# A gated unit whose output sums run over two chunks in PSUM, with moved small steps around it

## The chip, the cores and the metric

The kernel runs on one core of one Trainium2 chip. The metric is the device time of the whole program in microseconds; the median of three runs is 434.72 us (434.70 to 435.04). The core has five engines with their own instruction streams: TensorE (PE, matmuls), VectorE (DVE), ScalarE (ACT), GpSimd (POOL) and SyncE (SP, which here only issues DMAs). Engines wait for one another through semaphores; each takes its own instructions in order.

## The reference

Three stages follow one another, all in float32 at their borders. The gated unit, which the change is mostly about, is the last.

```
# 1 linear attention with a decaying state, per head (2 x 8 heads, 768 steps, 48 wide)
cur = (u * k_t) outer v_t
y_t = r_t @ (state + cur);  state = w * state + k_t outer v_t
# 2 top-1 mixture of experts on 1536 tokens of 384: 8 experts, 1024 wide, a capacity per expert
h = relu(x_e @ w1[e]);  out = gate * (h @ w2[e])
# 3 gated unit, d_ff = 1536
g = x @ w_gate;  val = x @ w_val
out = (g * sigmoid(g) * val) @ w_out
```

The unit's weights arrive as float64.

## The kernel before

**Attention.** The 1536 tokens are 12 tiles of 128. For tile i, SP loads r and k twice: transposed (`load_T`, three buffers) and by token (`load_rk`, three buffers). DVE multiplies the transposed pair by powers of the decay (`decay`, line 258, one multiplication of 128x1024 whose inputs are both in SBUF; for tile 0 in two halves). POOL does two multiplications of 128x384 per tile, again with both inputs in SBUF: `diag_pool` (r times k, line 263) and `keys_pool` (the keys for the state, line 267). `products(i)` issues both and then the load of the tile three ahead into the buffer that they read; `decayed(i)` issues the decay and the transposed load. DVE finishes the diagonal (`diag_u`, line 270, and `diag_sum`, line 275), ACT spreads it on the diagonals of a tile (`diag_act`, line 288), PE computes scores (line 299, into PSUM buffers of which there are three, two per tile), and DVE copies the scores under a mask into the same tile (`masked`, line 307). A short prologue, written out by hand, does tiles 0 to 2 in part; then a loop follows. In the loop some POOL products are told to wait for a decay (`behind`, an explicit dependency, with the reason that both read two operands in SBUF).

**Experts.** Loads of w1 and w2 are split into a high and a low part (fp32r) by ACT and DVE; PE multiplies.

**Gated unit.** `gated` runs over six chunks c of 256 hidden columns, over two pairs p of token groups (a group is 384 tokens), and over two halves f of a chunk: 24 blocks, which the text calls (c,p,f). A block computes gate and value for both groups of its pair from sums of inputs and sums of weights: eleven products of three fp32r matmuls (high by high, high by low, low by high), collected in four PSUM banks named pa, pb, pc, pd. In order they are: the first gate product (into pb, copied to pa by ACT, line 1263), S1 (into pd, copied to m5 by ACT, line 1271), S2 (onto pb; then DVE adds pb and m5 into pc, line 1276), two products onto pa (then SiLU on ACT), S3 (onto pb; then DVE adds pb and m5 into pd, line 1285), two onto pc (then SiLU, line 1291), one onto pd (then DVE multiplies by the gate, line 1297), two onto pb (then DVE multiplies, line 1303). Each result is split by `halves`: ACT casts the high part (line 1231), POOL subtracts to get the low part (line 1232; in the last block DVE does that). The second result of a block is split at the start of the next block.

The output sums of a chunk, three tiles of 128 tokens per group, are handed out as fill: `sum_tile` issues six matmuls (lines 1204 to 1206) for a tile, at up to three places of a block, before S1, before S3 and before the product onto pd; there is none at the first place until block (0,1,1). `added` (lines 1208 to 1219) then evicts the bank: ACT copies it for the first chunk, DVE adds it to a tile in SBUF for the others (line 1213), and after the last chunk POOL sends the rows out by an indirect DMA (line 1215). Only one set of tiles, group 2 of the second pair, is summed over the last two chunks in PSUM, with twelve matmuls each.

Beside this, the float64 weights of the coming chunk are converted in steps that `background` hands out (lines 828 to 921): DVE shifts and merges bits (lines 837, 843, 849), ACT casts the high part, POOL subtracts the low part (line 876). `STEPS` says how many of these steps, and how many of the second pair's input steps (`x_pair`, lines 1137 to 1176), a block takes at its three places. A step in the list takes its place in every engine's stream that it uses. After the last block `at_end` loads a flag (whether a rare case needs the general path) on every engine; the flag is made from PE's count in an output bank and one DVE operation (lines 1322 to 1330).

Of the kernel before, what the change touches and what calls it, by code (L numbers as in the profile page):

```python
# [74 lines left out]

class Kernel:
# [14 lines left out]
    def run(self):  # L91
        tc, nc = self.tc, self.nc
        with ExitStack() as top, tc.manual_schedule():
# [7 lines left out]
            with ExitStack() as ex:  # L101
# [10 lines left out]
                self.wff = [self.weights_ff(mp, 0)]  # L112
# [16 lines left out]
    def attention(self, st):  # L129
# [281 lines left out]
        def products(i):  # L411
            diag_pool(i)
            keys_pool(i)
            load_rk(i + NB)
# [9 lines left out]
        products(1)  # L424
        warm(WARMS[0])
        scores(0)
        decayed(1)
        load_v(3, 1)
# [7 lines left out]
        products(2)  # L436
# [5 lines left out]
        decayed(2)  # L442
        state_pe(1)
# [370 lines left out]
    def weights_ff(self, pool, i):  # L814

        shapes = {"in": [P, NW, 256], "out": [P, 2, DM]}
        return {m: [pool.tile(shape, F32R, name=f"w{m}_{q}{i}") for q in ("hi", "lo")] for m, shape in shapes.items()}
# [7 lines left out]
    def convert(self, m, c):  # L825
# [5 lines left out]
        wide = lambda: self.wff[c % 2]["in" if m != "w_out" else "out"]  # L831
# [305 lines left out]
    def x_pair(self, p):  # L1137
# [9 lines left out]
        def low(at, src, n):  # L1147
            nc.vector.tensor_sub(xl[:, at:at + n], src, xh[:, at:at + n].bitcast(F32))
# [28 lines left out]
    def gated(self, st, at_end=lambda: None):  # L1177
# [6 lines left out]
        self.wff.append(self.weights_ff(wk, 1))  # L1184
        self.xb.append(self.x_rooms(wk, 1))
# [4 lines left out]
        sums, todo = [], []  # L1190
# [3 lines left out]
            (0, 1, 0): ((0, 2), (0, 1), (0, 2)),  # L1194
        }

        def tile_of(c, n, parts):

            po = ps_o.tile([P, DM], F32, name="po", tag="po")
            ts_ = slice(n % NTT * P, (n % NTT + 1) * P)  # L1200
            for i, (at, f, halves_, j) in enumerate(parts):
                ah, al = halves_[j]
                wh, wl = (w[:, f] for w in self.wff[at % 2]["out"])
                nc.tensor.matmul(po, lhsT=ah[:, ts_], rhs=wh, start=(i == 0), stop=False)  # L1204
                nc.tensor.matmul(po, lhsT=ah[:, ts_], rhs=wl, start=False, stop=False)  # L1205
                nc.tensor.matmul(po, lhsT=al[:, ts_], rhs=wh, start=False, stop=(i == len(parts) - 1))  # L1206
            return lambda: added(c, n, po)

        def added(c, n, po):
            if c == 0:  # L1210
# [3 lines left out]
            if c == NC - 1:  # L1214
# [13 lines left out]
        def halves(sg, eng=nc.gpsimd):  # L1228
            h_ = wk.tile([P, TG], F32R, name="ah", tag="ah", bufs=12)
            l_ = wk.tile([P, TG], F32R, name="al", tag="al", bufs=12)  # L1230
            nc.scalar.copy(h_, sg)  # L1231
            eng.tensor_sub(l_, sg, h_.bitcast(F32))  # L1232
            return h_, l_

        def block(c, p, f, steps, tiles):
# [4 lines left out]
            room = lambda name: wk.tile([P, TG], F32, name=name, tag=name, bufs=2)  # L1240
# [6 lines left out]
            def product(ps, wi, xi, first=False):  # L1247
                wh, wl = (w[:, wi, fs] for w in self.wff[c % 2]["in"])
# [4 lines left out]
            def opened(ps):  # L1253

                if c == p == f == 0:
                    nc.tensor.matmul(
                        ps, lhsT=self.wff[0]["in"][0][:, GATE, fs], rhs=self.xb[0][0][:, X11], start=True, stop=True
                    )
# [41 lines left out]
            parts = [None, halves(gate1, low_eng)]  # L1300
# [4 lines left out]
            def rest():  # L1305
                parts[0] = halves(gate0, low_eng)
# [3 lines left out]

        prep, before = self.x_pair(1), []
        for c in range(NC):
            for p in range(2):
                blocks = [block(c, p, f, STEPS.get((c, p, f), ((0, 1), (0, 1), (0, 2))), c > 0 or p > 0 and f > 0) for f in range(2)]
# [7 lines left out]
                if c == NC - 1 and p == 1 and not self.guarded:  # L1322
                    how_many = ps_o.tile([P, DM], F32, name="po", tag="po")
                    nc.tensor.matmul(
                        how_many[:, 0:1], lhsT=self.ones_bf, rhs=low_any, start=True, stop=True
                    )
                    nc.vector.scalar_tensor_tensor(
                        out=self.rare_i, in0=how_many[0:1, 0:1], scalar=0.0, in1=self.rare_f,
                        op0=ALU.is_gt, op1=ALU.add,
                    )  # L1330
                for j in (1, 0):
                    parts = [(c, f, blocks[f], j) for f in range(2)]

                    if (p, j) == (1, 0) and c == NC - 2:
                        held = parts
                        continue
                    if (p, j) == (1, 0) and c == NC - 1:
                        parts = held + parts
                    sums += [(c, (2 * p + j) * NTT + tt, parts) for tt in range(NTT)]
        before.pop()()  # L1340
        while sums:
            if len(sums) == 1:
                at_end()
# [4 lines left out]
    def general(self):  # L1348
# [86 lines left out]
        self.wff, self.xb = self.wff[0:1], self.xb[0:1]  # L1435
# [58 lines left out]
```

## Time and profile before

| | us |
|---|---|
| median of 3 runs | 434.72 |
| profiled execution, its own time | 434.78 |
| its span, first to last instruction | 433.0 |
| PE busy in the span | 417.6 |
| DVE busy | 330.9 |
| ACT busy | 256.8 |
| POOL busy | 158.9 |

The profile is of one execution. Its time stands 0.06 us over the median of the runs; 1.8 us of it lie outside the span. PE's matmuls overlap in the records, so the distance from one start to the next says more than a duration. A hole in PE's work is a distance that is larger than that of its neighbours.

### The profile page before, as it was taken

The page shows a single profiled execution, that of the slowest core. Times are in us where ns is not written, and L with a number is a line of the kernel's source. Part 1 is how long each engine was busy: PE and PEld are TensorE (multiplying, and loading weights), DVE is VectorE, ACT ScalarE, POOL GpSimd, SP SyncE. Part 2 cuts the span into 40 slices and gives each one's busy share as a digit, 9 for nine tenths or more (in the row PEclk, how much of TensorE's full clock was granted, in tenths as well). Part 3 has the DMA queues.
Part 4 walks back from the last instruction along what each step waited for, and adds up shares of the span by engine and source line. Part 5 has one row for each costly group of instructions (what it writes and reads, how often), then busy time and mean ns, then how long its engine had stood idle before and what let it go on. Part 6 is the DMA issues. An engine that isn't in the chain of part 4 may idle for free. (4 is left out here: it accounts for less than half of the span.)

```text
span 433.0 us, 8410 instructions
## 1 busy us (share of the span) xinstructions
PE 417.6 (96%) x3105; PEld 401.1 (93%) x3105; DVE 330.9 (76%) x648; ACT 256.8 (59%) x557; POOL 158.9 (37%) x149
## 2 busy tenths in 40 slices
PE   8999999999999999999999999999999999999991
PEld 7888889999999999999899999999999999999981
DVE  6999996878788988888887578888779778543440
ACT  2688875565876777766766765466546555433300
POOL 5846643111021110000148544445436535323541
PEclk9999999999999999999999999999999999999996
DMA  7999933899999999503012121212221220000221
GB/s 262 350 339 341 408 123 107 246 308 335 326 294 271 260 286 252 193 1 75 0 62 73 52 79 37 88 52 78 75 78 62 75 73 2 0 2 0 74 108 47
DMA packets 23938, 63.78 MB, mean 147 GB/s; under 512 B 4816, under 2 KB 8272, under 8 KB 23888
## 3 DMA queue, kind: packets, MB, share of 16 engines
q1 hardware_dynamic: 21248, 57.43, 41.2%
q0 software_dynamic: 1920, 4.73, 3.0%
q10 hardware_dynamic: 720, 1.00, 1.0%
q8 instruction: 26, 0.43, 0.4%
q14 instruction: 24, 0.20, 0.1%
HBM read 55.67 MB, written 7.48 MB: 146 GB/s over the span
## 5 line engine op out<-in xcount | busy, mean ns | idle before, releaser
L1232 POOL TENSOR_TENSOR al<-gate,ah 128x384 fp32r<-128x384 f32 x46 | 49.8, 1086 | 141.4 <-ACT ah L1231 141.3
L753 DVE TENSOR_TENSOR wlo<-raw,whi 128x768 fp32r<-128x768 f32 x60 | 56.9, 957 | 10.8 <-ACT whi L752 9.4
L942 PE MATMUL py<-hc,whi 128*128 128x448 f32 x192 | 62.3, 379 | 0.0
L953 PE MATMUL A<-xc,whi 128*128 128x224 f32 x336 | 57.2, 276 | 0.3 <-DVE xc L769 0.3
L953 PEld LDWEIGHTS A<-xc,whi 128*128 128x128 f32 x336 | 51.0, 192 | 0.9 <-DVE xc L769 0.5
L943 PE MATMUL py<-hc,wlo 128*128 128x224 f32 x192 | 51.0, 266 | 0.0
L752 ACT CAST whi<-raw 128x768 fp32r<-128x768 f32 x60 | 49.7, 839 | 1.7 <-PE py L942 1.7
L1204 PE MATMUL po<-wout_hi,ah 128*128 128x384 f32 x144 | 48.7, 338 | 0.3 <-DVE x L1213 0.2
L1206 PE MATMUL po<-wout_hi,al 128*128 128x384 f32 x144 | 48.9, 340 | 0.0
L1205 PE MATMUL po<-wout_lo,ah 128*128 128x384 f32 x144 | 48.5, 337 | 0.0
L953 PE MATMUL A<-xc,wlo 128*128 128x224 f32 x168 | 45.9, 273 | 0.0
L1231 ACT CAST ah<-gate 128x384 fp32r<-128x384 f32 x48 | 24.7, 515 | 34.2 <-DVE gate L1297 33.1
L1251 PE MATMUL A<-xbh,win_hi 128*128 128x384 f32 x120 | 40.8, 340 | 1.1 <-DVE gc L1276 0.9
L1251 PE MATMUL A<-xbh,win_lo 128*128 128x384 f32 x120 | 40.3, 336 | 0.0
L1251 PE MATMUL A<-xbl,win_hi 128*128 128x384 f32 x120 | 40.3, 336 | 0.0
L1020 POOL DMA_INDIRECT ids<-tok,by_expert x12 | 13.9, 1156 | 69.8 <-DMA ids<-tok,by_expert 63.5
L942 PEld LDWEIGHTS py<-hc,whi 128*128 128x128 f32 x192 | 36.1, 188 | 3.0
L943 PEld LDWEIGHTS py<-hc,wlo 128*128 128x128 f32 x192 | 36.7, 191 | 0.0
L1213 DVE TENSOR_TENSOR x<-x,po 128x384 f32<-128x384 f32 x57 | 30.9, 544 | 6.7 <-PE po L1206 6.7
L972 ACT ACTIVATE hc<-A 128x224 fp32r<-128x224 f32 x64 | 23.2, 362 | 21.2 <-PE A L953 17.3
L288 ACT ACTIVATE AT<-ident,c 128x128 f32<-128x128 f32 x96 | 30.2, 393 | 4.6 <-DVE c L275 4.5
L953 PEld LDWEIGHTS A<-xc,wlo 128*128 128x128 f32 x168 | 32.3, 192 | 0.0
(208 smaller groups left out, 1070.9 us busy)
## 6 DMA issues: line engine op xcount, KB each, us to landing
raw<-in_w SPq DMA_DIRECT2D x62, 384.0 KB, 8.3
rkT<-in_rkT SPq DMA_DIRECT2D x12, 512.0 KB, 5.9
rk<-in_rk SPq DMA_DIRECT2D x12, 384.0 KB, 5.3
raw<-in_w_gate SPq DMA_DIRECT2D x6, 768.0 KB, 4.9
raw<-in_w_val SPq DMA_DIRECT2D x6, 768.0 KB, 4.3
raw<-in_w_out SPq DMA_DIRECT2D x6, 768.0 KB, 4.9
x_disp<-zero SPq DMA_DIRECT2D x8, 336.0 KB, 6.5
xr<-x_disp SPq DMA_DIRECT2D x8, 336.0 KB, 6.9
```

The costliest lines, as they stand in the source:

```text
L288: nc.scalar.activation(AT[i][:, j, hp], ident, AF.Copy, scale=cc[i][:, j, hp:hp + 1])
L752: nc.scalar.copy(h_, raw)
L753: nc.vector.tensor_sub(l_, raw, h_.bitcast(F32))
L942: nc.tensor.matmul(ps[:, 0:2 * BLK], lhsT=wh, rhs=xc, start=first, stop=False, skip_group_check=True)
L943: nc.tensor.matmul(ps[:, HI], lhsT=wl, rhs=xc[:, HI], start=False, stop=last, skip_group_check=True)
L953: self.nc.tensor.matmul(ph[:, HI], lhsT=w[:, k, fs], rhs=x[1][:, k, half], start=(k == 0 and i == 0), stop=(k == KD - 1 and i == 2),)
L1204: nc.tensor.matmul(po, lhsT=ah[:, ts_], rhs=wh, start=(i == 0), stop=False)
L1205: nc.tensor.matmul(po, lhsT=ah[:, ts_], rhs=wl, start=False, stop=False)
L1206: nc.tensor.matmul(po, lhsT=al[:, ts_], rhs=wh, start=False, stop=(i == len(parts) - 1))
L1213: nc.vector.tensor_add(acc[:, n], acc[:, n], po)
L1232: eng.tensor_sub(l_, sg, h_.bitcast(F32))
L1251: nc.tensor.matmul(ps, lhsT=w, rhs=x, start=first and i == 0, stop=False, skip_group_check=True)
```

## The change

Output sums: instead of one eviction per chunk, each group's tile stays open in PSUM over two chunks. `held(c, j)` says which group of a pair waits for the next chunk: the first of the pair after even chunks, the second after odd ones, none after the last. `sum_tile` now issues one piece, six matmuls of one chunk, and evicts after the last piece of a tile. The high and low parts of held groups get their own seven buffers each, the others four each in place of twelve; the output weights get three buffers instead of two, and m5 one instead of two.

Smaller parts: the low parts of the first block are kept back until the inputs of the second pair are split, with an explicit dependency on that split. In block (0,1,0) one conversion step moves from the second place to the third. The flag is made ahead of the last block, in one of the pa-tile banks. In the attention, `products(1)` and `products(2)` stand behind the decays of tiles 1 and 2, and their first product waits for them.

```diff
-        def products(i):
-            diag_pool(i)
+        def products(i, after=None):
+            op = diag_pool(i)
+            if after:
+                behind(op, after)
             keys_pool(i)
             load_rk(i + NB)
...
-        products(1)
         warm(WARMS[0])
         scores(0)
         decayed(1)
+        products(1, decays[1])
...
-        products(2)
         scores(1)
         outputs(0)
...
         decayed(2)
+        products(2, decays[2])
         state_pe(1)
         products(3)
...
-            (0, 1, 0): ((0, 2), (0, 1), (0, 2)),
+            (0, 1, 0): ((0, 1), (0, 2), (0, 2)),
...
+        def held(c, j):
+            return c % 2 == j and c < NC - 1
...
         def sum_tile():
-            if sums:
-                todo.append(tile_of(*sums.pop(0)))
+            if not sums:
+                return
+            c, n, pieces, i, end = sums.pop(0)
+            if i == 0:
+                opened_sum.append(ps_o.tile([P, DM], F32, name="po", tag="po"))
+            po = opened_sum[-1]
+            ts_ = slice(n % NTT * P, (n % NTT + 1) * P)
+            for f, (h_, l_) in enumerate(pieces[i][1]):
+                at = pieces[i][0]
+                wh, wl = (w[:, f] for w in self.wout[at % 3])
+                nc.tensor.matmul(po, lhsT=h_[:, ts_], rhs=wh, start=(i == 0 and f == 0), stop=False)
+                nc.tensor.matmul(po, lhsT=h_[:, ts_], rhs=wl, start=False, stop=False)
+                nc.tensor.matmul(po, lhsT=l_[:, ts_], rhs=wh, start=False, stop=(end and f == 1))
+            if end:
+                first, last = pieces[0][0] == 0, c == NC - 1
+                todo.append(lambda: added(n, po, first, last))
...
+        def halves(sg, eng, hold, long):
+            tags, bufs = (("kh", "kl"), 7) if long else (("ah", "al"), 4)
+            h_, l_ = (wk.tile([P, TG], F32R, name=t, tag=t, bufs=bufs) for t in tags)
             nc.scalar.copy(h_, sg)
-            eng.tensor_sub(l_, sg, h_.bitcast(F32))
+            low = lambda: eng.tensor_sub(l_, sg, h_.bitcast(F32))
+            held_lows.append(low) if hold else low()
...
+            hold = c == p == f == 0
+            if held_lows and not prep:
+                for low in held_lows:
+                    self.tc.add_manual_dep(
+                        low().ins, self.token_low.ins.name, AFTER, reason="both read two operands in SBUF"
+                    )
+                held_lows.clear()
+            long = [held(c, j) or (c, j) == (NC - 1, 0) for j in range(2)]
...
+        def flagged():
+            how_many = self.pa_tile()
+            nc.tensor.matmul(how_many[:, 0:1], lhsT=self.ones_bf, rhs=low_any, start=True, stop=True)
+            nc.vector.scalar_tensor_tensor(
+                out=self.rare_i, in0=how_many[0:1, 0:1], scalar=0.0, in1=self.rare_f, op0=ALU.is_gt, op1=ALU.add,
+            )
...
                 for j in (1, 0):
-                    parts = [(c, f, blocks[f], j) for f in range(2)]
...
+                    pieces = kept.pop((p, j), []) + [(c, Parts(blocks, j))]
+                    if held(c, j):
+                        kept[p, j] = pieces
                         continue
...
+                    for tt in range(NTT):
+                        sums += [(c, (2 * p + j) * NTT + tt, pieces, i, i == len(pieces) - 1) for i in range(len(pieces))]
```

`token_low` is the last low part that `x_pair` issued on DVE; `Parts` gives the parts of a chunk's two halves for one group of the pair.

## Rows read from the trace of the kernel before

**Rows 1.** The page: engines' busy time; a group of instructions by line.

```profile
PE 417.6 (96%) x3105; PEld 401.1 (93%) x3105; DVE 330.9 (76%) x648; ACT 256.8 (59%) x557; POOL 158.9 (37%) x149
...
L1213 DVE TENSOR_TENSOR x<-x,po 128x384 f32<-128x384 f32 x57 | 30.9, 544 | 6.7 <-PE po L1206 6.7
```

**Rows 2.** Windows: length, then PE, PEld, DVE, ACT, POOL busy, clock, DMA.

```profile
12.00:25.00 13.00, 12.20 (x179) 10.59 (x179) 12.93 (x24) 9.47 (x30) 10.12 (x11) 1.00 0.97 351
240.00:260.00 20.00, 20.00 (x117) 20.00 (x115) 12.52 (x19) 13.72 (x29) 9.05 (x7) 1.00 0.21 69
```

**Rows 3.** Timeline of PE in the gated unit: start, duration, instruction, idle before.

```profile
214.39 0.45 PE L1251 MATMUL A<-xbh,win_hi 128*128 128x384 f32 x1 [0.65 <-DVE gc L1276]
...
224.65 0.44 PE L1251 MATMUL gd<-xbh,win_hi 128*128 128x384 f32 x1 [0.20 <-DVE gd L1285]
...
414.38 0.44 PE L1204 MATMUL po<-wout_hi,ah 128*128 128x384 f32 x1
...
415.92 0.44 PE L1204 MATMUL po<-wout_hi,ah 128*128 128x384 f32 x1 [0.24 <-DVE x L1213]
```

**Rows 4.** Timeline of DVE in the attention's prologue.

```profile
10.24 1.61 DVE L258 TENSOR_TENSOR RK<-rkT,W 128x1024 f32<-128x1024 f32 x1
...
14.30 1.74 DVE L258 TENSOR_TENSOR RK<-rkT,W 128x1024 f32<-128x1024 f32 x1
...
17.38 0.73 DVE L307 COPY_PREDICATED AT<-mask,A 128x512 f32<-128x512 uint8 x1
...
18.73 1.21 DVE L258 TENSOR_TENSOR RK<-rkT,W 128x1024 f32<-128x1024 f32 x1
```

**Rows 5.** Timeline of POOL in the attention's prologue.

```profile
9.77 1.00 POOL L267 TENSOR_TENSOR kd<-rk,wk_tok 128x384 f32<-128x384 f32 x1 [0.62 <-ACT wk_tok L247]
10.73 1.99 POOL L263 TENSOR_TENSOR ruk<-rk 128x384 f32<-128x384 f32 x1
...
17.82 1.01 POOL L267 TENSOR_TENSOR kd<-rk,wk_tok 128x384 f32<-128x384 f32 x1
```

**Rows 6.** Timeline of ACT in the attention's prologue.

```profile
16.07 1.28 ACT L288 ACTIVATE AT<-ident,c 128x128 f32<-128x128 f32 x4
```

**Rows 7.** Timeline of PE in the attention, the scores of tile 3.

```profile
21.47 1.37 PE L299 MATMUL A<-RK 48*128 48x128 f32 x16
```

**Rows 8.** Timeline of several engines at blocks (0,0,1) and (0,1,0).

```profile
211.15 1.00 POOL L1232 TENSOR_TENSOR al<-gate,ah 128x384 fp32r<-128x384 f32 x1 [51.91 <-ACT ah L1231]
...
211.29 1.27 DVE L1161 TENSOR_TENSOR comb<-x 128x384 f32<-128x384 f32 x1
...
216.79 0.49 ACT L1291 ACTIVATE gate<-gc 128x384 f32<-128x384 f32 x1
...
217.43 0.55 DVE L1297 TENSOR_TENSOR gate<-gd,gate 128x384 f32<-128x384 f32 x1
...
218.15 0.34 PE L1251 MATMUL gd<-xbh,win_hi 128*128 128x384 f32 x1
...
218.97 0.45 PE L1251 MATMUL A<-xbh,win_hi 128*128 128x384 f32 x1
```

**Rows 9.** Timeline of several engines in block (0,1,1).

```profile
227.35 2.20 POOL L1232 TENSOR_TENSOR al<-gate,ah 128x384 fp32r<-128x384 f32 x2 [4.05 <-ACT ah L1231]
...
228.77 1.20 DVE L837 TENSOR_SCALAR bits<-raw 128x768 int32<-128x768 int32 x1
...
229.89 0.55 DVE L1276 TENSOR_TENSOR gc<-A,m 128x384 f32<-128x384 f32 x1
...
231.07 0.34 PE L1251 MATMUL A<-xbh,win_hi 128*128 128x384 f32 x1
...
231.09 3.14 POOL L876 TENSOR_TENSOR win_lo<-comb,win_hi 128x1024 fp32r<-128x1024 f32 x1
...
232.34 2.71 DVE L849 SCALAR_TENSOR_TENSOR bits<-raw,bits 128x768 int32<-128x768 int32 x1
```

**Rows 10.** The page: DMA issues by line, median us to landing last.

```profile
rk<-in_rk SPq DMA_DIRECT2D x12, 384.0 KB, 5.3
```

More of the change, by code (lines that the diff above doesn't have):

```diff
@@ L73, with __init__, __iter__ @@
 TINY2 = float(np.array([0x38100000], np.int32).view(np.float32)[0]) ** 2
+class Parts:
+    def __init__(self, blocks, j):
+        self.blocks, self.j = blocks, j
+    def __iter__(self):
+        return (b[self.j] for b in self.blocks)
 class Kernel:
@@ L814, in weights_ff, with weights_out @@
     def weights_ff(self, pool, i):
-        shapes = {"in": [P, NW, 256], "out": [P, 2, DM]}
-        return {m: [pool.tile(shape, F32R, name=f"w{m}_{q}{i}") for q in ("hi", "lo")] for m, shape in shapes.items()}
+        return [pool.tile([P, NW, 256], F32R, name=f"win_{q}{i}") for q in ("hi", "lo")]
+    def weights_out(self, pool, i):
+        return [pool.tile([P, 2, DM], F32R, name=f"wout_{q}{i}") for q in ("hi", "lo")]
     def x_rooms(self, pool, i):
@@ L830, in convert @@
         word = lambda raw, i: raw.rearrange("p (c two) -> p c two", two=2)[:, :, i]
-        wide = lambda: self.wff[c % 2]["in" if m != "w_out" else "out"]
+        wide = lambda: self.wff[c % 2] if m != "w_out" else self.wout[c % 3]
         def s0(raw):
@@ L1184, in gated @@
         self.wff.append(self.weights_ff(wk, 1))
+        self.wout += [self.weights_out(wk, i) for i in (1, 2)]
         self.xb.append(self.x_rooms(wk, 1))
@@ L1189, in gated, with added @@
         acc = self.x2.rearrange("p k n -> p (k n)")[:, 0:NT * DM].rearrange("p (t d) -> p t d", d=DM)
-        sums, todo = [], []
+        sums, todo, opened_sum, kept = [], [], [], {}
         STEPS = {
             (0, 0, 0): ((1, 0), (1, 0), (0, 0)), (0, 0, 1): ((1, 0), (2, 1), (1, 0)),
-            (0, 1, 0): ((0, 2), (0, 1), (0, 2)),
+            (0, 1, 0): ((0, 1), (0, 2), (0, 2)),
         }
[L1197 to L1210, printed above, removed]
+        def held(c, j):
+            return c % 2 == j and c < NC - 1
+        def added(n, po, first, last):
+            if first:
                 nc.scalar.copy(acc[:, n], po)
@@ L1313, in gated @@
             for p in range(2):
-                blocks = [block(c, p, f, STEPS.get((c, p, f), ((0, 1), (0, 1), (0, 2))), c > 0 or p > 0 and f > 0) for f in range(2)]
+                blocks = []
+                for f in range(2):
+                    if (c, p, f) == (NC - 1, 1, 1) and not self.guarded:
+                        flagged()
+                    steps = STEPS.get((c, p, f), ((0, 1), (0, 1), (0, 2)))
+                    blocks.append(block(c, p, f, steps, c > 0 or p > 0 and f > 0))
                 if c == 1 and p == 1:
@@ L1321, in gated @@
                     nc.vector.tensor_scalar(out=low_any, in0=low_sum, scalar1=0.0, scalar2=None, op0=ALU.is_gt)
[L1322 to L1330, printed above, removed]
                 for j in (1, 0):
-                    parts = [(c, f, blocks[f], j) for f in range(2)]
-                    if (p, j) == (1, 0) and c == NC - 2:
-                        held = parts
+                    pieces = kept.pop((p, j), []) + [(c, Parts(blocks, j))]
+                    if held(c, j):
+                        kept[p, j] = pieces
                         continue
-                    if (p, j) == (1, 0) and c == NC - 1:
-                        parts = held + parts
-                    sums += [(c, (2 * p + j) * NTT + tt, parts) for tt in range(NTT)]
+                    for tt in range(NTT):
+                        sums += [(c, (2 * p + j) * NTT + tt, pieces, i, i == len(pieces) - 1) for i in range(len(pieces))]
         before.pop()()
         while sums:
-            if len(sums) == 1:
+            if len(sums) == 2:
                 at_end()
```

22 lines of the change are left out of this document (10 added, 12 removed).

## The prediction

> **What bounds the kernel now.** I read the page's engine line first: TensorE (PE) is busy for 417.6 of 433.0 us, and VectorE (DVE), the next, for 330.9 [rows 1]. A busy PE may still be waiting, so I went on to the windows by stage. In the attention (12 to 25 us) DVE is busy for 12.93 of 13.00 us while PE runs small tiles; deep in the gated unit (240 to 260 us) PE is full and DVE has 12.52 of 20 us [rows 2]. There 117 matmuls take 20.00 us, 0.171 us each. So a product (three matmuls) is 0.52 us of PE and a piece of an output sum (six) 1.03 us. The gated unit is then a stream of matmuls whose number the change leaves alone; only holes in the stream and what follows the last matmul can move the end. In PE's timeline from 204 to 424 us I looked for starts further apart than 0.174 us. The holes that matter here stand at 214.39, 224.65, 414.38 and 415.92 [rows 3]. After a hole the second matmul also starts 0.11 us late.
>
> **Adds halved.** 69 evictions become 42: 12 ScalarE (ACT) copies as before and 30 DVE adds instead of 57. That takes 27 x 0.544 = 14.7 us from DVE [rows 1]. It is worth nothing by itself: DVE had 7.5 us free in 20 [rows 2], and the matmuls stay. What changes is when they run. A held half gives no pieces, so block (0,1,1) has one piece for its three places and block (1,0,1) none, where before each had three. These five pieces (5.2 us) run later; 11 instead of 9 pieces' worth stand behind the last product. A block with pieces hides its evictions behind 1.03 us of PE each; without them PE meets whatever DVE and ACT are late with.
>
> **Low parts kept back.** The GpSimd (POOL) low part at 211.15 ends at 212.15; the DVE subtraction issued at 211.29 takes 1.27 us and ends 0.41 us after it [rows 8], though the same shape takes 0.55 us elsewhere in the stage. So a DVE operation with both inputs in SBUF and a POOL one exclude each other. Without that, DVE is ready in time and PE's hole of 0.81 + 0.11 us at 214.39 [rows 3] closes. What is late next: the first product of block (0,1,0) writes the bank that DVE's gate product at 217.43 must have read, and that waits for ACT's SiLU at 216.79, at the end of ACT work without a gap, which does not move [rows 8]. Due 0.92 us earlier, that PE product can start only at about 217.9, some 0.24 us earlier than before, and 0.11 goes on the restart. I take a gain of 0.13 us (ends 0 and 0.92).
>
> **Order of the conversion steps in (0,1,0).** One step fewer stands ahead of the add that PE waits for at 224.65: 0.36 + 0.11 = 0.47 us gained [rows 3].
>
> **Where pieces are missing.** In (0,1,1) DVE does a shift of the weights' bits at 228.77 (1.20 us, behind POOL low parts that end at 229.55) and only then the add at 229.89; then another bit step, the next add, and at 232.34 a step of 2.71 us behind POOL's 3.14 us split [rows 9]. This chain hardly moves: its start, the gate product of the block before, hangs on ACT behind the same bit steps. Before, PE's next use of that bank came at 231.07 [rows 9]. After, it is due 0.60 us earlier by the two gains so far and 1.03 earlier by the missing piece: near 229.4. With POOL first at the port, as at 228.77, I follow the chain to an add that ends at 230.6: 1.3 + 0.1 us of hole, and behind the next add 0.75 us. If DVE got the port first, both together would be about 0.65. Between 0.65 and 2.15 I take 1.7, nearer the row's order. Two more products have nothing ahead of them to cover ACT's copy of the bank. The nearest rows are 218.15 and 218.97: the product there starts 0.82 us after the one ahead of it, which is 0.52 us of work, and restarts 0.11 late [rows 8]; with ACT free a little sooner I take 0.39 in (1,0,0) and 0.38 in (1,0,1). Costs: 1.7 + 0.77 = 2.5 us.
>
> **The end.** The flag moved ahead of the last block frees an output bank, and two pieces of older data stand before the sums that need the last low parts. The holes at 414.38 (0.35 + 0.10) and 415.92 (0.40 + 0.12) go [rows 3]: 1.0 us. The seven kept buffers are full in the last block: its last cast waits for one more piece, but 6 us of pieces stand before its reader, so I cost that at nothing; without that cover it would be 1.03 us. m5 with one buffer and the third output weight: nothing, their readers are a block or more away. After the last matmul come one add, one indirect DMA and its landing, as before. So the gated unit: 2.5 - 0.13 - 0.47 - 1.0 = 0.9 us longer.
>
> **First products wait.** The DVE decay at 10.24 took 1.61 us, and one with the port free 1.21 (18.73) [rows 4]. It waited for the key product kd(0), 9.77 to 10.77 [rows 5], and not for the product that is moved: that one (10.73) was itself held until the decay ended at 11.85 [rows 4, 5]. So products(1) gains nothing by waiting, and loses some 0.22 us: 0.09 for the signal, and its start-up, which used to run while it was held. DVE's next step needs it, and the sums and ACT's diagonals behind it go back by 0.22. The second decay (14.30, 1.74 us) is freed: it starts 0.22 late and ends 15.73 instead of 16.04. But ACT's diagonal (16.07, ends 17.35) is also 0.22 late, and DVE's masked copy at 17.38 starts right when it ends [rows 4, 6]. So the third decay asks at 18.95 instead of 18.73. POOL meanwhile runs four products from 15.82 at 0.96 us each (9.77 to 10.73 [rows 5]): the fourth, kd(3), which is not told to wait, starts at 18.70, 0.25 us ahead of the decay. Before, it had ended by 18.83 [rows 5]. The decay then starts on the port at 19.7 and ends at 20.81 instead of 19.94: 0.87 us. DVE is full here [rows 2], and PE's sixteen score matmuls at 21.47 already wait within for the masked copy behind this decay [rows 7]. From there PE runs almost without a hole, so I carry 0.85 us to the end. Ends: 0.31 gained (if the freed decay counted whole), 0.87 lost. The loads moved: rkT(4) goes out some 2 us sooner, rk(4) about 0.3 later at 14.0; at 5.3 us to landing [rows 10] it is there by 19.5, before its product at 21 or later.
>
> The Trainium skill ("SBUF — State Buffer", "Who interferes with whom") says that issue order decides who blocks, and that the loser waits out the whole instruction. The rows at 10.24 and 211.29 agree: each DVE operation ended about a clean duration after POOL's. By this rule the 0.25 us lead of kd(3) decides: with the order turned, the attention costs 0.22 instead of 0.87 us.
>
> **Sum.** +0.85 + 0.9 = 1.75 us on the profiled execution's 434.78 us (433.0 span), which is 0.06 above the median of the runs. Predicted: 436.5 us.
>
> **Rivals.**
> 1. The order at the port turns, both in the attention (+0.2) and in (0,1,1) (0.65): 0.2 + 0.65 + 0.77 - 1.6 = 0.0, so 434.7 us. For it: leads of 0.25 and 0.1 us. Against: POOL was ahead in the rows of before.
> 2. Faster: the chain of conversions keeps pace with PE. Then the hole at 214.39 is regained whole and (0,1,1) costs nothing: 0.92 + 0.47 + 1.0 - 0.77 = 1.6 us, and with the freed decay's 0.31 reaching PE, 1.9: 432.8 us. It decides at ACT's SiLU at 216.79: if it comes 0.7 us sooner, all behind it does. For it: ACT has less to do, as eviction copies fall away in chunk 0. Against: ACT has no gap before that SiLU, and no copy stands there.
> 3. The halved adds free PE directly, which is what the change says it does. Then the holes behind a DVE add of an output go and nothing else moves. Of the holes only 415.92 names one, for 0.24 us [rows 3]: 434.5 us, no difference that shows. I count it with the first.
>
> **How the numbers follow.** My forecast has 0.48 (its own range 435.6 to 437.6), the even case 0.25, the faster one 0.27. About half the faster case lies below 432.7. A collision at every place, with only the end gained, gives 0.87 + 2.15 + 0.77 - 1.0 = 2.8 us more, 437.5. The range is 432.7 to 437.6. A difference under 0.2% (0.87 us) cannot be told from none; faster 0.27, same 0.25, slower 0.48.
>
> **What would show it.** DVE's third whole decay with 2 us instead of 1.21, beside kd(3); PE's score matmuls near 22.4. Around 214 no hole on a DVE add, but one before the first product of (0,1,0). In (0,1,1) holes of 1.4 and 0.75 us before products that follow DVE adds. From the last product on no hole on DVE. It is wrong if the decay takes 1.2 us, if (0,1,1) runs without holes, or if new holes appear in later chunks, where I expect none.

## The result and the profile after

The changed kernel takes 438.02 us (median of 6 runs, 437.70 to 438.18) against 434.75 for the kernel before beside it (6 runs, 434.51 to 435.04): 1.0069 times as long, 95% interval [1.0059, 1.0079]. The direction was the one forecast; the time lies 1.5 us above the 436.5 and 0.4 us above the end of the range. The profiled execution has a span of 436.4 us against 433.0. One execution of a later experiment (pairs, steps fitted) took 1536.14 us, in a slow state, and is left out of that run's median.

First the page of the kernel after, the busy time of the engines, and the group of output adds from its lines view (busy us, mean ns, then the idle time before them):

```profile
PE 418.1 (96%) x3105; PEld 400.6 (92%) x3105; DVE 317.2 (73%) x621; ACT 256.2 (59%) x557; POOL 159.9 (37%) x149
```

```profile
L1219 DVE TENSOR_TENSOR x<-x,po 128x384 f32<-128x384 f32 x30 | 16.4, 546 | 6.0 <-PE po L1239 6.0
```

Against [rows 1] the adds are 27 fewer and DVE has 13.7 us less to do, 1 us short of the forecast; PE's busy time is the same within 0.5 us. The relief shows nowhere in the time.

Where the time went is read from PE's timeline. Two rows cut the run into stretches that can be compared between kernels: the S2 product of block (0,0,1), the second block, which comes after the same 0.25 us hole in every kernel here, and the last matmul. Kernel before, then after (start, duration, instruction):

```profile
211.91 0.44 PE L1251 MATMUL A<-xbh,win_hi 128*128 128x384 f32 x1
...
423.23 0.34 PE L1206 MATMUL po<-wout_hi,al 128*128 128x384 f32 x1
```

```profile
212.67 0.44 PE L1274 MATMUL A<-xbh,win_hi 128*128 128x384 f32 x1
...
218.69 0.44 PE L1274 MATMUL gd<-xbh,win_hi 128*128 128x384 f32 x1 [0.52 <-DVE gate L1320]
...
228.69 0.44 PE L1274 MATMUL A<-xbh,win_hi 128*128 128x384 f32 x1
...
231.49 0.44 PE L1274 MATMUL A<-xbh,win_hi 128*128 128x384 f32 x1 [0.94 <-DVE gc L1299]
...
233.46 0.44 PE L1274 MATMUL gd<-xbh,win_hi 128*128 128x384 f32 x1
...
235.66 0.34 PE L1237 MATMUL po<-wout_hi,ah 128*128 128x384 f32 x1
...
237.09 0.44 PE L1237 MATMUL po<-wout_hi,ah 128*128 128x384 f32 x1 [0.75 <-ACT ah L1253]
...
238.18 0.44 PE L1239 MATMUL po<-wout_hi,al 128*128 128x384 f32 x1 [0.47 <-POOL al L1254]
...
247.06 0.44 PE L1274 MATMUL A<-xbh,win_hi 128*128 128x384 f32 x1
...
426.54 0.34 PE L1239 MATMUL po<-wout_hi,kl 128*128 128x384 f32 x1
```

Up to the first of these rows ("arrival") the kernel after is 0.76 us later. From there to the last matmul ("gated stretch") it takes 213.87 us instead of 211.32: 2.55 us more. Behind the start of the last matmul 9.77 and 9.86 us are left. Within the gated stretch the gaps above 0.174 us between starts answer to the forecast thus: the 0.92 us at 214.39 [rows 3] are gone and 0.68 + 0.11 stand at 218.69 instead (net gain 0.13, forecast 0.13); the one at 224.65 [rows 3] is gone (0.47); the two at the end are gone (0.98, forecast 1.0). In (0,1,1) stand 0.20 at 228.69, 1.21 at 231.49 and 0.40 at 233.46: 1.8 us, forecast 1.7. At 247.06 stands ACT's copy in (1,0,1), 0.37, forecast 0.38. And at 237.09 and 238.18 stand 1.03 and 0.75 us, inside the first piece of block (1,0,0), which begins at 235.66; there the forecast had 0.39 for a copy.

What that piece waits for, from the timelines of DVE, ACT and POOL of the kernel after, and last the same gate product on DVE in the kernel before:

```profile
229.75 1.21 DVE L850 TENSOR_SCALAR bits<-raw 128x768 int32<-128x768 int32 x1
230.88 0.55 DVE L1299 TENSOR_TENSOR gc<-A,m 128x384 f32<-128x384 f32 x1
...
233.31 2.72 DVE L862 SCALAR_TENSOR_TENSOR bits<-raw,bits 128x768 int32<-128x768 int32 x1
235.95 0.55 DVE L1320 TENSOR_TENSOR gate<-gd,gate 128x384 f32<-128x384 f32 x1
...
236.53 0.51 ACT L1253 CAST ah<-gate 128x384 fp32r<-128x384 f32 x1 [2.68 <-DVE gate L1320]
...
232.06 3.16 POOL L889 TENSOR_TENSOR win_lo<-comb,win_hi 128x1024 fp32r<-128x1024 f32 x1
237.12 1.01 POOL L1254 TENSOR_TENSOR al<-gate,ah 128x384 fp32r<-128x384 f32 x1 [1.91 <-ACT ah L1253]
```

```profile
234.97 0.55 DVE L1297 TENSOR_TENSOR gate<-gd,gate 128x384 f32<-128x384 f32 x1
```

DVE's last bit step of w_out takes 2.72 us beside POOL's split of 3.16; the gate product of (0,1,1) stands right behind it on DVE, at 235.95. The piece has two halves of three matmuls. The first half reads the parts of (0,1,0), which are at hand; the second reads those of (0,1,1). So the fourth matmul waits for ACT's cast at 236.53 (0.75 us of idle on it), and the sixth for POOL's low part of 1.01 us (0.47). In the kernel before the gate product comes 23.06 us behind the arrival, here 23.28: the chain has hardly moved. But before, an older piece stood in this place of (1,0,0), and PE had no wait there.

The attention, from the timelines of DVE, POOL and PE after:

```profile
10.64 1.22 DVE L267 TENSOR_TENSOR RK<-rkT,W 128x1024 f32<-128x1024 f32 x1
...
14.51 1.22 DVE L267 TENSOR_TENSOR RK<-rkT,W 128x1024 f32<-128x1024 f32 x1
...
17.59 0.74 DVE L316 COPY_PREDICATED AT<-mask,A 128x512 f32<-128x512 uint8 x1 [0.20 <-ACT AT L297]
...
18.94 1.85 DVE L267 TENSOR_TENSOR RK<-rkT,W 128x1024 f32<-128x1024 f32 x1
...
18.70 1.01 POOL L276 TENSOR_TENSOR kd<-rk,wk_tok 128x384 f32<-128x384 f32 x1
...
21.68 0.48 PE L308 MATMUL A<-RK 48*128 48x128 f32 x2
22.53 1.16 PE L308 MATMUL A<-RK 48*128 48x128 f32 x14 [0.36 <-DVE AT L316]
```

Against [rows 4] the second whole decay takes 1.22 instead of 1.74 us, the masked copy is 0.21 late, and the third decay, asked for 0.24 us after kd(3) has begun, takes 1.85 instead of 1.21: from the end of the first whole decay on, all as forecast. That the two profiles can be compared from there is luck. In this execution the first half decay starts at 7.39, 0.38 us later than in that of the kernel before (7.01), but the first whole decay at 10.64 meets no POOL product, takes 1.22 us where [rows 4] has 1.61, and ends within 0.01 us of the one there. Of the scores of [rows 7], two matmuls start at 21.68 and the other fourteen, behind the masked copy, at 22.53.

### The profile page after: what moved, and what is told of

Its sections match the earlier page's. It is cut to its first block, busy times and chain, and to the rows that moved or that the text cites. A ratio compares the mean times of both kernels' runs of the same rounds, so it can differ in the third digit from the quotient of the medians.

```text
span 436.4 us, 8377 instructions
## 1 busy us (share of the span) xinstructions
PE 418.1 (96%) x3105; PEld 400.6 (92%) x3105; DVE 317.2 (73%) x621; ACT 256.2 (59%) x557; POOL 159.9 (37%) x149
## 5 line engine op out<-in xcount | busy, mean ns | idle before, releaser
L1254 POOL TENSOR_TENSOR al<-gate,ah 128x384 fp32r<-128x384 f32 x23 | 25.7, 1118 | 108.8 <-DVE xbl L1161 58.4
L1254 POOL TENSOR_TENSOR kl<-gate,kh 128x384 fp32r<-128x384 f32 x23 | 25.4, 1106 | 33.0 <-ACT kh L1253 32.9
L1320 DVE TENSOR_TENSOR gate<-gd,gate 128x384 f32<-128x384 f32 x24 | 13.3, 556 | 30.1 <-PE gd L1274 26.3
L1299 DVE TENSOR_TENSOR gc<-A,m 128x384 f32<-128x384 f32 x24 | 13.5, 561 | 20.8 <-PE A L1274 20.8
L1253 ACT CAST ah<-gate 128x384 fp32r<-128x384 f32 x24 | 12.3, 514 | 25.0 <-DVE gate L1320 25.0
L1308 DVE TENSOR_TENSOR gd<-A,m 128x384 f32<-128x384 f32 x24 | 13.5, 564 | 17.8 <-PE A L1274 17.7
```

The source lines that it names most:

```text
L1254: low = lambda: eng.tensor_sub(l_, sg, h_.bitcast(F32))
L1299: nc.vector.tensor_add(pc, pb, m5)
L1308: nc.vector.tensor_add(pd, pb, m5)
```

## The experiments

All times are medians, the ratio is to the kernel before on the same chip. "Arrival" and "gated" are the two readings above, from one profile each; "gated" was within 0.05 us for kernels that share that code (213.82 to 213.87 in three with the change, 211.28 and 211.32 in two without), and decides where a ratio doesn't.

| run | us | ratio, 95% | arrival | gated |
|---|---|---|---|---|
| before | 434.75 | | 211.91 | 211.32 |
| after | 438.02 | 1.0069 [1.0059, 1.0079] | 212.67 | 213.87 |
| after, attention of before | 437.28 | 1.0032 [1.0009, 1.0055] | 212.01 | 213.86 |
| before, attention of after | 435.42 | 1.0002 [0.9986, 1.0019] | 212.32 | 211.28 |
| after, products(2) not waiting | 437.18 | 1.0042 [1.0023, 1.0061] | 211.71 | 213.82 |
| pairing alone | 437.58 | 1.0057 [1.0044, 1.007] | 212.24 | 213.90 |
| small parts alone | 434.93 | 1.0002 [0.9993, 1.0012] | 212.18 | 211.17 |
| flag alone | 435.52 | 1.0016 [1.0002, 1.003] | 213.20 | 211.42 |
| after, a step out of (0,1,1) | 436.40 | 1.0018 [1.0002, 1.0034] | 212.94 | 212.27 |
| after, old attention, holes filled | 437.48 | 1.0063 [1.0049, 1.0077] | 212.40 | 213.90 |
| pairs from chunk 1 | 439.23 | 1.0096 [1.008, 1.0112] | 212.24 | 214.78 |
| pairs, steps moved | 434.90 | 1.0 [0.9989, 1.001] | 211.89 | 211.23 |
| no pairs, (4,1,0) in order | 433.75 | 0.9983 [0.9972, 0.9994] | 212.28 | 210.15 |
| no pairs, steps moved | 433.61 | 0.9979 [0.9968, 0.999] | 211.87 | 210.00 |
| no pairs, steps fitted | 432.22 | 0.993 [0.9903, 0.9957] | 212.90 | 209.00 |
| pairs, steps fitted | 434.95 | 0.9996 [0.9976, 1.0016] | 212.06 | 211.37 |
| pairs at the end | 431.62 | 0.9932 [0.9918, 0.9945] | 211.90 | 208.28 |

"No pairs" is the kernel before with the small parts. The ratio is taken over all executions, also those with a lower mean clock, and so need not be that of the medians. Among the executions with a mean granted clock of 0.991 or more ("undisturbed"; the last section says why) the medians differ from that of the kernel before by +2.57 us (after, attention of before), +0.71 (before, attention of after), +2.48 (pairing alone), -0.17 (small parts alone), -2.42 (no pairs, steps fitted) and -3.12 (pairs at the end). All but the second lie within 0.1 us of the change in the gated stretch.

**The attention.** Three runs: the changed kernel with the old place of the two products, the kernel before with the new one, and the changed kernel with one of the two waits.

```diff
-        products(1, decays[1])
-        products(2, decays[2])
+        products(1)       # each at its old place: after, attention of before
+        products(2)       # this one alone, at its new place: products(2) not waiting
```

> The changed kernel with the attention as before (products(1) and products(2) back in their old places, without waits). Theory T: the wait of the first products costs 0.75 to 0.85 us, because the fourth POOL product then holds the port when DVE's third decay asks for it, so 437.2 us, and PE's matmuls from 100 us on start as early as before. Rival: the loss is all in the gated unit and the decay's 0.6 us beside POOL is made up later, so 438.0 us.

> The kernel before with only the attention's part of the change. Theory T: 0.8 us slower than before, 435.5 us, with the third whole decay at 1.85 us and the gated unit as before but later. Rival: within 0.2 us of before, 434.7 us.

> The changed kernel in which products(2) stands in its new place, but its first product does not wait for the decay. Theory T (the port): the products run one step sooner, the fourth ends at about 18.9 us when the third decay asks, the decay takes 1.2 us, the second decay 1.5 us: 437.3 us. Rival (order of the loads on SP, which stays as in the changed kernel, or the place of products(1)): 438.0 us.

Undoing it gives 437.28, 0.74 us less than the changed kernel; done alone it gives 435.42. The ratio of that run can't be told from 1; among the undisturbed executions it is 0.71 us slower (12 against 22). Arrival says the same: 211.87 to 212.40 with the old attention (eleven runs of the table, without the two at 213.20 and 212.90, for which see the end), 212.32 to 212.94 with both waits (three): 0.55 us between the means, each of single executions. Counted from the start of the first half decay (6.92 to 7.39), which takes out part of what the loads ahead differ by, it is 0.49. With products(2) not waiting, the timelines of DVE and POOL read:

```profile
14.12 1.85 DVE L267 TENSOR_TENSOR RK<-rkT,W 128x1024 f32<-128x1024 f32 x1
...
18.64 1.21 DVE L267 TENSOR_TENSOR RK<-rkT,W 128x1024 f32<-128x1024 f32 x1
...
13.89 1.00 POOL L272 TENSOR_TENSOR ruk<-rk 128x384 f32<-128x384 f32 x1 [0.39 <-DMA rk<-in_rk]
...
17.75 0.99 POOL L276 TENSOR_TENSOR kd<-rk,wk_tok 128x384 f32<-128x384 f32 x1
```

Without its wait the product at 13.89 again stands 0.23 us ahead of the second decay, which takes 1.85; kd(3) comes at 17.75, 0.9 us ahead of the third decay, which takes 1.21. (I had expected 1.5 for the second.) So the wait of products(2) moves the collision from the second decay, where ACT's diagonals covered it, to the third, where nothing does. That issue order decides who waits out whom (the Trainium skill, "SBUF — State Buffer", "Who interferes with whom") fits both rows: leads of 0.23 and 0.24 us each cost a whole 0.6 us.

**Which part of the change costs.** The pairing alone (low parts, order of steps and flag as before), the small parts alone (no pairing), and the flag alone, all with the old attention:

```diff
-            return c % 2 == j and c < NC - 1      # small parts alone: this and all of the pairing is left out
-            hold = c == p == f == 0
+            hold = False                           # pairing alone
-            (0, 1, 0): ((0, 1), (0, 2), (0, 2)),
+            (0, 1, 0): ((0, 2), (0, 1), (0, 2)),   # pairing alone
-                    if (c, p, f) == (NC - 1, 1, 1) and not self.guarded: flagged()
+                if (c, p) == (NC - 1, 1) and not self.guarded: flagged()   # pairing alone; the flag alone is the reverse, in the kernel before
```

> The changed kernel with the pairing alone: old attention, no low parts kept back, old order of the steps in (0,1,0), the flag at its old place. Theory (the chain of conversions doesn't move, so PE's 1.4 us of holes at 214 and 224 come back and are taken off the holes at 231 and 233, which were waits for that chain): against 437.28 us of the changed kernel with the old attention +0 to +0.9, for the end: 437.3 to 438.2. Rival (parts and pairing add up): 437.28 + 0.14 + 0.47 + 1.0 = 438.9.

> The kernel before with the small parts of the change alone: low parts of block (0,0,0) kept back, the conversion steps of (0,1,0) in the new order, the flag ahead of the last block; no pairing, old attention. Theory (these three are worth what the holes say, 0.14 + 0.47 + up to 1.0 us, and with pieces in every place the blocks behind hide the chain): 434.8 - 0.6 - (0.5 to 1.0) = 433.2 to 433.7. Rival (the chain of conversions takes the 0.6 us back in (0,1,1), since it doesn't move, and the end's second hole stays without the pairing's older pieces): 434.3 to 434.8.

> The kernel before with the flag ahead of the last block and nothing else. Theory (the flag's own bank caused the hole at 414.4, the missing older pieces the one at 415.9): 0.45 us gained, the hole at 415.9 stays: 434.35. Rival (the flag caused both): 433.8. Second rival (the end is set by something else): 434.8.

The gated stretch grows by 2.58 us with the pairing alone and shrinks by 0.15 with the small parts alone, where my theory had 1.1 to 1.6 us gained. In this stretch the pairing is the whole cost. PE's timeline at the end, of the small parts alone and then of the pairing alone:

```profile
413.96 0.44 PE L1206 MATMUL po<-wout_hi,al 128*128 128x384 f32 x1
...
416.03 0.44 PE L1204 MATMUL po<-wout_hi,ah 128*128 128x384 f32 x1 [0.57 <-DVE x L1213]
```

```profile
414.59 0.44 PE L1237 MATMUL po<-wout_hi,kh 128*128 128x384 f32 x1
```

With the flag moved and no pairs the first hole of the end shrinks to 0.24 and the second grows to 0.85 (0.74 + 0.11): nothing gained. With the pairs and the flag at its old place 0.27 is left of 1.0. So some 0.7 of the gain comes from the pairs' older pieces alone; the bank that the flag frees gains nothing by itself, and the last 0.27 goes only with both. The flag alone has a median 0.4 us above that of the kernel before beside it (435.12), but not by its gated stretch, which is that of before within 0.1: the difference lies ahead of it (last section).

**Is the missing piece the cause, or the conversions beside it?** One conversion step out of (0,1,1) into (1,0,0); twelve matmuls that nobody reads into the two empty places of (0,1,1); and the first pair one chunk later (with it all parts share one set of 11 buffers). The third entry of a block in `STEPS` is the one that it hands out first, behind S1; so the step moves behind the gate products of (0,1,1), to the place that (1,0,0) takes first, although the expectation of a later run calls it the last.

```diff
+            (0, 1, 1): ((0, 1), (0, 0), (0, 2)), (1, 0, 0): ((0, 1), (0, 1), (0, 3)),   # a step out of (0,1,1)
...
             sum_tile()
+            cover(c, p, f)                                    # holes filled: six matmuls, twice
...
-            return c % 2 == j and c < NC - 1
+            return c % 2 == j and 0 < c < NC - 1              # pairs from chunk 1
```

> The changed kernel with one conversion step (the last bit step of the output weights, 2.7 us on DVE) moved from block (0,1,1) into (1,0,0). Theory T: the holes of 0.92 + 0.11 + 0.64 + 0.11 us at 237 to 238 us, where the first piece of (1,0,0) waits for the parts of the block just ahead, hang on the gate product behind that step; the product comes 1.5 us sooner and the holes go: 436.3 us. Rival: pieces that are missing in (0,1,1) and (1,0,1) cost what they cost wherever the steps stand, and the hole only moves into (1,0,0): 437.9 us or slower.

> The changed kernel with the attention of before, and with two pieces of idle work (twice six matmuls into an output bank that nobody reads) in the two empty places of block (0,1,1). Nothing else differs. Theory (the length of a block without pieces is set by the conversions behind it, so the holes at 231, 233, 236 and 237, 3.5 us with their restarts, are only time in which PE waits for them): the 2.06 us of added matmuls fall into the holes, which shrink by as much; 437.3, at most 437.6. Rival (PE is the bound there, and each added matmul lengthens the run): 437.28 + 2.06 = 439.3.

> The changed kernel with the attention of before, and with no half of chunk 0 held: the pairs run (1,2), (3,4) at one half and (2,3), (4,5) at the other, so chunk 0 has all its pieces and 48 evictions instead of 42 remain (the parts of all results share one set of 11 buffers). Theory (what costs is that the pieces are missing exactly where the conversions run behind, in the blocks (0,1,1) to (1,0,1)): the holes at 231.5, 233.5, 237.1, 238.2 and 247.1 go, 3.8 us with their restarts, from 437.28 us of the changed kernel with the old attention; the blocks of chunk 1 and 2 that now lack pieces cost 0 to 0.9 us instead: 433.5 to 434.4. Rival (a block without pieces costs the same wherever it stands, ACT's copy and DVE's eviction always being late): 437.3.

The step moved gives 436.40 (gated 1.60 us less). DVE's gate product of (0,1,1) then comes 21.69 us behind the arrival instead of 23.28, and of the two holes in the first piece of (1,0,0) only 0.20 us is left. PE's timeline of this run:

```profile
236.88 0.44 PE L1240 MATMUL po<-wout_hi,al 128*128 128x384 f32 x1
```

The holes in (0,1,1) stay, 1.11 + 0.11 and 0.30 + 0.11 us, with 0.12 ahead of them, so what this step cost was the wait in (1,0,0).

The idle matmuls cost nothing: 2.06 us more of PE's work, and the gated stretch stays at 213.90 against 213.86. PE's timeline of the run with them:

```profile
230.09 1.21 PE L1250 MATMUL po<-wout_hi,kh 128*128 128x384 f32 x6
231.22 0.44 PE L1282 MATMUL A<-xbh,win_hi 128*128 128x384 f32 x1
...
232.90 1.22 PE L1250 MATMUL po<-wout_hi,kh 128*128 128x384 f32 x6
233.95 0.33 PE L1282 MATMUL gd<-xbh,win_hi 128*128 128x384 f32 x1
...
236.84 0.45 PE L1237 MATMUL po<-wout_hi,ah 128*128 128x384 f32 x1
...
237.92 0.44 PE L1239 MATMUL po<-wout_hi,al 128*128 128x384 f32 x1 [0.46 <-POOL al L1262]
```

The idle matmuls run from 230.09 and 232.90. Without them (the run with the old attention, whose rows I move by the 0.39 us between the arrivals) the products behind would start at 231.23 and 233.20, and the first piece of (1,0,0) would have its two late matmuls at 236.84 and 237.92. Here the four stand at 231.22, 233.95, 236.84 and 237.92: the first filling costs nothing, the second 0.75 us, and by the first piece all is as it was. PE waits there for a chain that doesn't hurry.

Moving the missing pieces one chunk on was a miss for both theories: 439.23, with a gated stretch 0.9 us longer than with pairs from chunk 0. (Two of its five executions are undisturbed, 438.19 and 438.48; the rival's 437.3 is the nearer.) The holes stand at the same places one chunk later, 0.53, 1.88, 1.04 and 1.11 us between 266 and 275 and 0.36 at 283; the longest in PE's timeline:

```profile
269.57 0.44 PE L1274 MATMUL gd<-xbh,win_hi 128*128 128x384 f32 x1 [1.60 <-DVE gd L1308]
```

My slack in chunk 1 wasn't there: its blocks too have four conversion steps each.

**Fitting the steps.** The order 1, 2, 1 of the entries for (4,1,0) without pairs; with it no step ahead of the second SiLU in (0,0,1), caught up in (1,0,0); then one step instead of two ahead of the first eviction of (0,1,1) (here the add of pb and m5 into pc). Beside them the same for the pairing.

```diff
+            (4, 1, 0): ((0, 1), (0, 2), (0, 1)),                                     # all five
-            (0, 0, 1): ((1, 0), (2, 1), (1, 0)),
+            (0, 0, 1): ((1, 0), (2, 0), (1, 0)), (1, 0, 0): ((0, 1), (0, 1), (0, 3)), # no pairs moved; both fitted
+            (0, 1, 1): ((0, 2), (0, 1), (0, 1)),                                     # both fitted
+            (0, 1, 1): ((0, 1), (0, 0), (0, 2)), (1, 0, 0): ((0, 1), (0, 1), (0, 3)), # pairs, steps moved
```

> As the run without pairs before it, with the move in (4,1,0) alone. Theory: the holes at 365 and 368 lose 0.5 to 1.0 us of 1.02: 433.9 to 434.4. Rival (the holes only shift): 434.9.

> The kernel before with the small parts (low parts kept, order in (0,1,0), flag), no pairing, old attention, and three moves of conversion steps: none at the second place of (0,0,1), whose ACT work stands ahead of the SiLU that PE waits for at 218 us; one more at the last place of (1,0,0), to catch up; the order 1, 2, 1 in (4,1,0). Theory: the holes at 218.2 and 219.1 (0.80 + 0.41 us) lose 0.5 to 0.9, those at 365 and 368 (0.54 + 0.48) 0.5 to 1.0; from 434.9 us to 433.0 to 433.9. Rival (the step that is late by one place makes a hole of its own in (0,1,0) or (0,1,1), where the chain has just kept pace): 434.5 to 435.5.

> The pairing with everything that the runs so far found: old attention, one conversion step moved out of (0,1,1) to the last place of (1,0,0), and in (4,1,0) the steps in the order 1, 2 with one in the last place, as the order in (0,1,0). Theory (the holes are program order of conversion steps against products, each can be moved by itself): 437.28 - 1.6 for the first move and - 0.5 to - 1.0 for the holes at 363 and 366 (0.56 + 0.48 us with their restarts): 434.7 to 435.2, even with before. Rival (the steps of (4,1,0) only shift their holes to the next place): 435.7.

> The same steps without the pairing. Theory (the hole of 0.91 + 0.10 us at 230.5 was two steps ahead of one eviction): it goes, and at most 0.5 us of it comes back before the gate product: 433.61 - 0.5 to 1.0 = 432.6 to 433.1. Rival (the step that runs late makes the hole wherever it stands): 433.6.

> The pairing with old attention and the conversion steps fitted to it: none at the second place of (0,0,1), one instead of two ahead of the first eviction in (0,1,1), one more at the end of (1,0,0), and the order 1, 2, 1 in (4,1,0). Theory (pieces that come later cost only what the conversions then leave open, so with the steps out of PE's way the pairing costs the copies in (1,0,0) and (1,0,1), 0.5 us, against a gain of 0.9 us at the end): the holes at 217.9 (0.80) and 230.7 and 232.7 (1.24 + 0.40) of the run with the steps moved shrink to 0.5 us or less together, 434.9 - 1.9 = 433.0 or less, down to 432.5. Rival (the conversions of (0,1,1) take longer than the block without pieces, in whatever order, so that what is gained at 218 is lost at 231, as without pairs): 434.4 to 434.9.

The order in (4,1,0) is worth 1.02 us of gated stretch, as expected. The step taken from (0,0,1) closes the 0.8 us at 218 and opens 1.0 at 230.5 (theory and rival both half right, 0.15 net); one step fewer ahead of that eviction closes this too (1.00 us of gated stretch, the top of the expected 0.5 to 1.0; the time of 432.22 us lies below the expected range). Without pairs the stretch is then 209.00 us, 2.32 less than before. With pairs the same steps give 211.37; the best with pairs is 211.23. PE's timeline with pairs and fitted steps:

```profile
231.30 0.44 PE L1276 MATMUL gd<-xbh,win_hi 128*128 128x384 f32 x1 [0.84 <-DVE gd L1310]
...
234.15 0.45 PE L1239 MATMUL po<-wout_hi,ah 128*128 128x384 f32 x1
...
236.11 0.44 PE L1241 MATMUL po<-wout_hi,al 128*128 128x384 f32 x1 [1.33 <-POOL al L1256]
```

The holes have moved, not gone: 1.11 us on an eviction into pd, and 0.25 and 1.61 in the first piece of (1,0,0), for POOL's low part. So my theory for this run fell. Moved steps gain 2.6 us with pairs (213.86 to 211.23 at best) and 2.3 without (211.32 to 209.00); the cost of the pairing at this place stays, 2.2 to 2.7 us in each order of the steps that was run (213.86 against 211.17 with the small parts, 211.23 and 211.37 against 209.00 fitted).

**Pairs where nothing is converted.** From the fitted kernel without pairs, both groups of the second pair of chunk 4 held for chunk 5 (as in the kernel before, one of them was already):

```diff
-                    if (p, j) == (1, 0) and c == NC - 2:
-                        held = parts
+                    if p == 1 and c == NC - 2:
+                        held[j] = parts
```

> The run without pairs and with fitted steps (432.2 us), with one pair more: both halves of group 1 of chunk 4 are held and summed with chunk 5's in one bank (before, one half of it was). Three adds fewer; the three missing pieces fall on the blocks (5,0,0) and (5,0,1), where no conversion runs any more and DVE is idle for over half the time; each last sum begins with 1.03 us of products of the older chunk. Theory (a missing piece costs what the conversions behind it leave open, so here only ACT's copies of a bank, up to 0.4 us in each of the two blocks, against up to 0.9 us of the 0.27 + 0.85 us of holes at 412 and 414): from the first product of the second block to the last matmul 209.0 us becomes 208.1 to 208.9; 431.3 to 432.1. Rival (a missing piece costs the same 0.5 us and more wherever it stands, as the five did in chunk 0): 209.6 or more; 432.8 or more.

431.62 us, 0.9932 [0.9918, 0.9945] of before: the fastest, and 0.72 us of gated stretch under the kernel it is made from. PE's timeline has this hole in the blocks that lack pieces, and the holes at the end, 0.24 and 0.85 us, are gone:

```profile
384.70 0.45 PE L1256 MATMUL A<-xbh,win_hi 128*128 128x384 f32 x1
...
420.18 0.34 PE L1208 MATMUL po<-wout_hi,al 128*128 128x384 f32 x1
```

0.37 us at 384.70, one copy by ACT, is all that the missing pieces cost here. The empty places are as many as with the pairs from chunk 0, and stand alike: two in (5,0,0) and three in (5,0,1), of which two were empty already, against two in (0,1,1) and three in (1,0,1). There they cost 4 us. And the first piece of (5,1,0), made of the newest parts like that of (1,0,0), waits 0.23 us, as it did without the pair.

## Why the prediction was wrong

- **What bounds, and what the halved adds bring** were right: 13.7 us of DVE freed, nothing gained; what the gated stretch lost is found in holes of PE.
- **The attention**: mechanism right in each row; 0.5 to 0.76 us by the readings, forecast 0.85; this hides a little of what the gated unit cost more. The first whole decay's 1.61 us, from which I worked, is not the rule: 6 of the 11 profiles with the old attention that "arrival" counts have it at 1.21 to 1.33.
- **Low parts, order of steps**: 0.13 and 0.47 us as forecast in the changed kernel's holes (the product that waits at 218.69 is S1, into pd, and not the first one, as I wrote), but next to no part of the total. The chain of conversions doesn't move when PE comes sooner; without pairs the small parts give 0.15 us in all, and with pairs 0.04 (213.90 to 213.86).
- **Where pieces are missing** is the step that failed. (0,1,1) came out at 1.8 us for 1.7 and (1,0,1) at 0.37 for 0.38. But (1,0,0) was priced at 0.39, for ACT's copy, as if its piece were at hand; it cost 1.78. With the old pieces used up, half of the first piece in its first place is made of the newest parts, those of (0,1,1)'s own result, and these hang on the gate product behind the bit step that I had listed at 232.34 [rows 9]. I followed that chain as far as the evictions and not to the next reader of what it makes. This term was 1.4 us too small, and moving that step away gave 1.60 us back. That is most of the 1.65 us by which the 0.9 of the gated unit fell short of 2.55, and more than the 0.4 us by which the time left the range; the rest is 0.1 us in (0,1,1) and changes below 0.1 in holes of later chunks.
- **The end**: 0.98 us gained, forecast 1.0. Some 0.7 of it is the pairs' own; that the flag frees a bank gained nothing without them.
- **The rivals**: neither the turned order nor the faster chain came; the worst case that I summed, 437.5, lacked the same term.

Left open: where between 0.5 and 0.76 us the attention's cost lies, since the loads ahead move the start by some tenths (first half decay at 6.91 to 7.39), and whether the wait of products(1) is worth anything. The run in which only it waits is level with the old attention (437.18 and 437.28), but there products(2) has its new place too.

## What to carry to other kernels

Work held back for later must be replaced at the place it leaves: list which operands the next work in that place needs, and how old they are, before pricing it at nothing. Delay pieces where no other engine works behind them (the last chunk: 0.7 us gained), not where a chain of conversions has just kept pace (from chunk 0: 2.2 to 2.7 us lost). Compare kernels by stretches between like instructions; that told 0.15 us from 2.6 where run times scatter by more.

## What the runs showed that I had not expected

PE's clock can fall in the attention. In the run with the flag alone, windows of 1 us (length, then PE, PEld, DVE, ACT, POOL busy, granted clock, DMA share, GB/s) read:

```profile
15.00:16.00 1.00, 0.06 (x5) 0.00 (x1) 1.00 (x2) 1.00 (x4) 1.00 (x1) 1.00 1.01 394
19.00:20.00 1.00, 1.00 (x18) 0.82 (x17) 1.00 (x2) 1.00 (x5) 0.09 (x1) 0.50 0.96 384
21.00:22.00 1.00, 1.00 (x16) 0.80 (x14) 1.00 (x2) 0.00 (x0) 1.00 (x2) 0.73 0.95 338
22.00:23.00 1.00, 1.00 (x18) 0.81 (x16) 1.00 (x4) 0.02 (x1) 0.33 (x1) 1.00 1.02 381
```

PE had stood idle for 0.94 us before 16.00, behind a decay that took 2.05 us on the port; some 2 us later the granted clock is 0.50, the 1.2 GHz level, for about 3 us, with PE busy throughout, and then 1.00 again. This execution arrives at 213.20 instead of about 212.1, and the profile of the fitted kernel without pairs shows the same (arrival 212.90). The hole alone does not decide it: four other profiles have the same hole of 0.93 or 0.94 us, and the clock stays at 1.00. The run without pairs and with steps moved, in the same view:

```profile
15.00:16.00 1.00, 0.17 (x8) 0.05 (x3) 1.00 (x2) 1.00 (x4) 1.00 (x1) 1.00 1.05 415
19.00:20.00 1.00, 1.00 (x26) 0.95 (x28) 1.00 (x2) 1.00 (x4) 0.00 (x0) 1.00 1.02 382
```

What decides it, no run here shows. The two profiles with the fall have a mean clock of 0.988, the other fifteen 0.992 to 0.995 and none; so I take executions at 0.991 or more as undisturbed. Of the fitted kernel these are 4 of 6, 432.10 to 432.23 us, and of the kernel before beside it 8 of 17, 434.37 to 435.09: 0.994 between the medians. The rest of the ratio of 0.993 comes from the others.
